# Loading K in 16 KB runs, and turning it in 1 KB pieces so that each batch comes out contiguous

## The chip, the core and the metric

The kernel runs on one core of one Trainium2 chip. The metric is the device time of one execution in microseconds (us), over repeated executions. Before the change it is 192.17 us, the median of three runs (192.04 to 192.22). The results are checked against the reference in every run.

## The reference

It is one decode step, one token for each of 4 batches, through two pairs of layers that share their weights: attention over a window of the cache, then a gated unit called GLU here.

```python
B, D = 4, 512;  Hq, Hkv, Sk, Dh = 32, 8, 8192, 128;  F = 1792      # all tensors bf16

def _A_ref(x, k_cache, v_cache, wq, wo):
    W = min(4096, max(256, Sk // 4))                               # 2048 positions
    q = (x @ wq) ...                                               # 4 query heads for each K/V head
    k = jnp.repeat(k_cache[:, :, Sk - W:, :], rep, axis=1)
    v = jnp.repeat(v_cache[:, :, Sk - W:, :], rep, axis=1)
    scores = jnp.einsum("bhqd,bhkd->bhqk", q, k) * (Dh ** -0.5)
    o = jnp.einsum("bhqk,bhkd->bhqd", _softmax(scores), v)
    return o ... @ wo

def _B_ref(x, w_gate, w_up, w_down):
    return (_sigmoid(x @ w_gate) * (x @ w_up)) @ w_down

x = x + _A_ref(_layernorm(x), ...);  x = x + _B_ref(_layernorm(x), ...)
x = x + _A_ref(_layernorm(x), ...);  x = x + _B_ref(_layernorm(x), ...)   # the same weights and caches
```

Two facts matter. The second attention needs the same K as the first, so K is loaded once (8 heads x 4 batches x 0.5 MB = 16.8 MB) and stays in SBUF. V is used twice; only its last few tiles can be kept, and the others are loaded twice.

## The kernel before

SBUF is one arena of 50 slots of 4 KB a partition. A slot holds one tile of 512 KB: K or V of one head and batch, or a piece of a weight. K takes 32 slots for good. The others are streaming buffers: SyncE issues the next load as soon as a slot comes free. A planner in Python fixes the order of the instructions on each engine. Each K tile is loaded in packets of 4 KB and turned in place on VectorE, 1024 four-byte words wide (one word is two bf16 values; the code lays K out in blocks of 32 words):

```python
def k_transpose(pairs):                    # pairs: one head, four batches = one "unit"
    for (h, b) in pairs:
        s = need(("K", h, b))
        v32 = slot_ap(s).bitcast(F32)                              # 128 x 1024 words
        P.op("vector", ..., lambda v, v32=v32: v.transpose(v32, v32),
             r=[("slot", s)], w=[("slot", s)])
```

TensorE reads the turned K with a step of 4 bytes, because both halves of each word stay together:

```python
    kt = slot_ap(ks[gi]).rearrange("p (j c k t) -> p c t j k", c=2, k=32, t=2)
    ... pe.matmul(ps[...], qbd[...], kt[:, cp // 2, cp % 2, :, :], ...)
```

The softmax then takes the maximum on VectorE, the exponential on ScalarE, reorders the result on TensorE and turns it on VectorE in one transpose of 128x256 words. The number of V tiles that stay from the first attention to the second is a constant:

```python
    KEEP_V = cfg.get("KEEP_V", 3)
    ...
    keep = set(seq[len(seq) - KEEP_V:])
```

A unit of the first attention turns the next K, multiplies q with K, does the softmax, multiplies with V, and frees the four V slots. SyncE fills them again.

Of the kernel before, what the change touches and what calls it, by code (L numbers as in the profile page):

```python
# [15 lines left out]
class _Op:  # L16
    __slots__ = ("idx", "eng", "name", "dur", "emit", "deps", "users", "start", "finish",
                 "sem", "val", "inc", "dma_bytes", "dma_rate", "waits", "prio", "ndeps_left")

    def __init__(self, idx, eng, name, dur, emit):  # L20
# [16 lines left out]
        self.ndeps_left = 0  # L37


class _Plan:  # L40
# [8 lines left out]
    def op(self, eng, name, dur, emit, r=(), w=(), banks=(), dma_bytes=0, dma_rate=0.0, after=()):  # L49
        o = _Op(len(self.ops), eng, name, dur, emit)  # L50
        o.dma_bytes = dma_bytes
# [32 lines left out]
def _schedule(ops, tm):  # L84
# [19 lines left out]
    while nleft:  # L104
        best = None
        best_key = None
        for e in ENGINES:
# [11 lines left out]
            for o in cand:  # L119
                t = ef  # L120
                for d in o.deps:
                    td = d.finish + sem_lat
                    if td > t:
                        t = td
                ests.append((t, o))
                if tmin is None or t < tmin:
                    tmin = t
            pick = None
            for x in ests:
                if x[0] <= tmin + tol and (pick is None or x[1].prio < pick[1].prio):  # L130
                    pick = x
            key = (pick[0], pick[1].prio)
# [114 lines left out]
class _SlotPool:  # L247
# [16 lines left out]
    bw_4k=412.0, bw_3k=409.0, bw_1k=356.0,  # L264
# [6 lines left out]
def build(nc, A_x, A_k, A_v, A_wq, A_wo, B_wg, B_wu, B_wd, out, cfg=None):  # L271
# [5 lines left out]
    KEEP_V = cfg.get("KEEP_V", 3)  # L277
# [20 lines left out]
    FCC = SLOT // D  # L298

# [12 lines left out]
    with es:  # L312
# [3 lines left out]
        arena = sb("arena", [128, NS * SLOT], BF16)  # L316
# [33 lines left out]
        pool = _SlotPool(NS)  # L350
        SB = (0, 1)
# [3 lines left out]
        CB = 7  # L355

        def slot_ap(s):
            return arena[:, s * SLOT:(s + 1) * SLOT]
# [4 lines left out]
        def c_act(n):  # L363
            return tm["act_fix"] + n * tm["act_el"]

# [13 lines left out]

        def take_load():  # L380
            name, emit = loads.pop(0)
# [4 lines left out]
        def fill():  # L386
            while loads and pool.free:
                take_load()

# [7 lines left out]

        def load_kv(name, cache, b, h):
            loads.append((name, lambda s: dma(str(name), slot_ap(s), kv_d(cache, b, h), w=[("slot", s)])))

        def load_cols(name, dram, n, rate):
            loads.append((name, lambda s: dma(str(name), slot_ap(s)[:, 0:n], dram, w=[("slot", s)], rate=rate)))

        def load_rows(name, dram, k, rate):
            loads.append((name, lambda s: dma(
                str(name), slot_ap(s)[:, 0:k * D].rearrange("p (f n) -> p f n", n=D), dram,
                w=[("slot", s)], rate=rate)))
# [47 lines left out]

        def add_weights(kind, k, only=None):
            chs = chunks[kind]
            if kind == "wq" and k:
# [170 lines left out]
        def k_transpose(pairs):  # L629
            for (h, b) in pairs:  # L630
                s = need(("K", h, b))
                v32 = slot_ap(s).bitcast(F32)
                P.op("vector", "T%d_%d" % (h, b), c_dve(1024), lambda v, v32=v32: v.transpose(v32, v32),  # L633
                     r=[("slot", s)], w=[("slot", s)])
# [3 lines left out]
        def softmax_unit(tag, pairs):  # L638
# [5 lines left out]
            ks = [where[("K", h, b)] for (h, b) in pairs]  # L644
            q_unit(tag, int(tag[0]), pairs[0][0], k2)

            def e_s(pe):
                last = None
                for cp in range(4):
                    for gi, (h, b) in enumerate(pairs):  # L650
                        kt = slot_ap(ks[gi]).rearrange("p (j c k t) -> p c t j k", c=2, k=32, t=2)
                        q0 = ((k2 * NB + b) * 4 + cp) * NR
                        last = pe.matmul(ps[32 * gi:32 * gi + NR, bank, :], qbd[:, q0:q0 + NR],  # L653
                                         kt[:, cp // 2, cp % 2, :, :], start=(cp == 0), stop=(cp == 3))
                return last
            P.op("tensor", "S" + tag, 16 * tm["pe_row"], e_s,
                 r=[("slot", s) for s in ks] + [("q", k2, a) for a in range(4)],
# [12 lines left out]
                 lambda a: a.activation(prow[:, :].rearrange("p (j k t) -> p j t k", k=32, t=2),  # L670
                                        ps[:, bank, :].rearrange("p (j t k) -> p j t k", k=32, t=2), ACTF.Exp, bias=nmax[:, 2 + k2:3 + k2], scale=1.0,
# [4 lines left out]
        def turn_p(tag, k2):  # L676
# [7 lines left out]
                 lambda v: v.transpose(ebuf[:, k2 * 256:(k2 + 1) * 256], prow[:, :].bitcast(F32)),  # L684
# [72 lines left out]
        def attn(L, gi_, wb):  # L757
# [6 lines left out]
            def front(ui):  # L764
# [3 lines left out]
                if L == 2:  # L768
                    for p in us[ui]:
                        done(("K",) + p)  # L770
# [22 lines left out]
        def glu(k, b0, b1):  # L793
# [181 lines left out]
```

## Time and profile before

| what | value | read from |
|---|---|---|
| time | 192.17 us (span of the profiled run 190.2) | the runs |
| DMA engines busy | 9 tenths in all slices but the first and the last | the span in 40 slices |
| main DMA queue | 72.37 MB, 97.9% of 16 engines' span | queue table |
| VectorE busy | 88.3 us, 46% | busy table |
| one K transpose, 1024 words | 1226 ns, 32 of them | groups |
| one softmax transpose, 256 words | 442 ns, 16 of them | groups |

These are lines of the profile's page of the kernel before. In the busy table each engine has its busy time, share and instructions. The digits are the busy tenths of 40 equal slices. The queue has packets, MB and its share of the 16 engines' span. The chain is what ended last, followed backwards. In the groups the columns are line, engine, operation, output<-input, shapes, count, then busy us and mean ns of one, then the idle us just before these instructions and what ended most of it.

```profile
...
PE 103.1 (54%) x1920; PEld 58.0 (30%) x1920; DVE 88.3 (46%) x220; ACT 33.3 (18%) x91; POOL 13.8 (7%) x73
...
DVE  6136998486582854729410023122584443311421
...
DMA  4999999999999999999999999999999999999990
...
q1 hardware_dynamic: 23392, 72.37, 97.9%
...
SPq 52%; DMA 29%; PE 10%; issue 4%; DVE 3%; ACT 2%; ACTq 0%
...
L718 PE MATMUL ps<-ebuf,arena 128*128 128x4 bf16 x1024 | 34.3, 167 | 15.6 <-DMA arena<-in_A_v_cache_dram 10.9
L633 DVE STREAM_TRANSPOSE arena<-arena 128x1024 f32<-128x1024 f32 x32 | 38.6, 1226 | 0.6 <-DMA arena<-in_A_k_cache_dram 0.2
...
L684 DVE STREAM_TRANSPOSE ebuf<-prow 128x256 f32<-128x256 f32 x16 | 7.1, 442 | 8.4 <-ACT prow L681 8.3
...
```

The DMA line and the queue's 97.9% say that the DMA engines are the bound. The chain agrees: 52% of it is SyncE's queue issuing loads and 29% is landings. TensorE's products with V (L718) wait 10.9 us for V to land.

### The profile page before, as it was taken

How to read it: one execution, taken by the hardware profiler on the slowest of the kernel's cores; microseconds unless marked ns; L12 is line 12 of the kernel's file. 1: busy time of each engine (PE TensorE's matmuls, PEld its weight loads, DVE VectorE, ACT ScalarE, POOL GpSimd, SP SyncE). 2: the span in 40 equal slices, each digit the busy share in tenths (PEclk: the TensorE clock that was granted, in tenths of full speed). 3: DMA queues.
4: the chain of work that ended last, by engine and by line, in shares of the span. 5: the costliest groups of instructions: out<-in, count | busy, mean ns of one | idle time of the engine just before them, and what ended most of it. 6: DMA issues, size and time to landing. Idle time of an engine off the chain costs nothing.

```text
span 190.2 us, 4466 instructions
## 1 busy us (share of the span) xinstructions
PE 103.1 (54%) x1920; PEld 58.0 (30%) x1920; DVE 88.3 (46%) x220; ACT 33.3 (18%) x91; POOL 13.8 (7%) x73
## 2 busy tenths in 40 slices
PE   0443322655517264171654436445979999966543
PEld 0110000232404123041234331321355555655122
DVE  6136998486582854729410023122584443311421
ACT  2010011430303003030020000000373333310100
POOL 3000001110101001010010000000022111100000
PEclk9999999999999999999999999999995555555555
DMA  4999999999999999999999999999999999999990
GB/s 133 344 416 410 408 410 389 409 394 404 407 390 411 391 405 412 388 409 394 400 393 389 407 405 371 397 337 409 409 409 408 402 410 406 408 408 405 403 365 16
DMA packets 23412, 72.66 MB, mean 382 GB/s; under 512 B 2264, under 2 KB 6368, under 8 KB 23392
## 3 DMA queue, kind: packets, MB, share of 16 engines
q1 hardware_dynamic: 23392, 72.37, 97.9%
q8 instruction: 15, 0.25, 0.5%
q14 instruction: 5, 0.04, 0.1%
HBM read 72.36 MB, written 0.00 MB: 381 GB/s over the span
## 4 chain that ended last, share of the span: by engine, by line
SPq 52%; DMA 29%; PE 10%; issue 4%; DVE 3%; ACT 2%; ACTq 0%
SPq L369 51%; DMA arena<-in_A_v_cache_dram 13%; DMA arena<-in_B_w_down_dram 11%; DMA arena<-in_A_wq_dram 5%; PE ps L653 3%; PE ps L718 2%; ACT prow L670 1%; PE ps L808 1%; PE ps L679 1%; PE ps L840 1%; DVE nmax L661 1%; PE ps L580 1%; PE ps L748 1%; DVE ebuf L684 0%; DVE ebuf L588 0%
## 5 line engine op out<-in xcount | busy, mean ns | idle before, releaser
L653 PE MATMUL ps<-arena,qbd 128*16 128x512 bf16 x256 | 28.7, 594 | 30.3 <-DVE arena L633 26.5
L718 PE MATMUL ps<-ebuf,arena 128*128 128x4 bf16 x1024 | 34.3, 167 | 15.6 <-DMA arena<-in_A_v_cache_dram 10.9
L633 DVE STREAM_TRANSPOSE arena<-arena 128x1024 f32<-128x1024 f32 x32 | 38.6, 1226 | 0.6 <-DMA arena<-in_A_k_cache_dram 0.2
L718 PEld LDWEIGHTS ps<-ebuf,arena 128*128 128x128 bf16 x1024 | 31.4, 104 | 23.8 <-DMA arena<-in_A_v_cache_dram 21.8
L670 ACT ACTIVATE prow<-ps,nmax 128x512 bf16<-128x512 f32 x16 | 13.3, 829 | 42.7 <-DVE nmax L667 41.3
L653 PEld LDWEIGHTS ps<-arena,qbd 128*16 128x16 bf16 x256 | 6.4, 109 | 44.1 <-DVE arena L633 27.1
L730 DVE TENSOR_TENSOR onb<-ps,rinv 128x16 bf16<-128x16 f32 x16 | 3.1, 192 | 35.5 <-PE ps L718 35.4
L661 DVE TENSOR_REDUCE nmax<-ps 128x1 f32<-128x512 f32 x16 | 10.9, 683 | 15.3 <-PE ps L653 15.3
L621 ACT CAST qbd<-ps 32x64 bf16<-32x64 f32 x32 | 6.5, 203 | 48.7 <-DVE qbd L618 48.4
L580 PE MATMUL ps<-arena,xn 128*4 128x512 bf16 x64 | 9.3, 576 | 9.4 <-DMA arena<-in_A_wq_dram 6.5
L688 POOL CAST s<-psm 128x1 bf16<-128x1 f32 x16 | 3.0, 187 | 146.9 <-ACT prow L670 146.9
L679 PE MATMUL ps<-prow,perm 128*128 128x512 bf16 x16 | 9.0, 563 | 5.4 <-ACT prow L670 5.2
L681 ACT CAST prow<-ps 128x512 bf16<-128x512 f32 x16 | 9.4, 586 | 9.5 <-PE ps L679 9.5
L684 DVE STREAM_TRANSPOSE ebuf<-prow 128x256 f32<-128x256 f32 x16 | 7.1, 442 | 8.4 <-ACT prow L681 8.3
L748 PE MATMUL ps<-onb,arena 128*128 128x4 bf16 x256 | 9.3, 166 | 2.9 <-DVE onb L730 1.5
L808 PE MATMUL ps<-arena,xn 128*4 128x448 bf16 x64 | 7.3, 556 | 6.4 <-DMA arena<-in_B_w_up_dram 3.5
L618 DVE CAST qbd<-ps 32x64 bf16<-32x64 f32 x32 | 6.8, 212 | 5.1 <-ACT qbd L621 3.8
L748 PEld LDWEIGHTS ps<-onb,arena 128*128 128x128 bf16 x256 | 8.2, 104 | 3.2 <-issue 2.9
L547 ACT ACTIVATE lnv<-lnv 128x4 f32<-128x4 f32 x4 | 0.8, 206 | 39.3 <-DVE lnv L544 39.3
L588 DVE STREAM_TRANSPOSE ebuf<-ps 128x512 f32<-128x512 f32 x4 | 2.9, 714 | 9.8 <-PE ps L580 9.8
L840 PE MATMUL ps<-hT,arena 128*128 128x4 bf16 x112 | 4.2, 167 | 4.3 <-DVE hT L830 2.2
L815 DVE STREAM_TRANSPOSE ebuf<-ps 128x448 f32<-128x448 f32 x4 | 2.6, 650 | 7.9 <-PE ps L808 7.9
(55 smaller groups left out, 61.8 us busy)
## 6 DMA issues: line engine op xcount, KB each, us to landing
arena<-in_A_v_cache_dram SPq DMA_DIRECT2D x61, 512.0 KB, 12.6
arena<-in_A_k_cache_dram SPq DMA_DIRECT2D x32, 512.0 KB, 13.1
arena<-in_A_wq_dram SPq DMA_DIRECT2D x16, 512.0 KB, 8.6
arena<-in_A_wo_dram SPq DMA_DIRECT2D x8, 512.0 KB, 15.0
arena<-in_B_w_gate_dram SPq DMA_DIRECT2D x8, 448.0 KB, 13.9
arena<-in_B_w_up_dram SPq DMA_DIRECT2D x8, 448.0 KB, 13.7
arena<-in_B_w_down_dram SPq DMA_DIRECT2D x6, 512.0 KB, 10.2
arena<-in_B_w_down_dram SPq DMA_DIRECT2D x2, 256.0 KB, 10.3
```

The lines of the kernel that those rows point to most:

```text
L369: o = P.op("sync", name, 0.0, lambda e, dst=dst, src=src: e.dma_start(dst, src), r=r, w=w, dma_bytes=nbytes, dma_rate=tm[rate])
L580: last = pe.matmul(ps[32 * hh:32 * hh + NB, qb, :], xn[:, c * NB:(c + 1) * NB], slot_ap(s)[:, hh * 512:(hh + 1) * 512], start=(c == 0), st ...
L633: P.op("vector", "T%d_%d" % (h, b), c_dve(1024), lambda v, v32=v32: v.transpose(v32, v32), r=[("slot", s)], w=[("slot", s)])
L653: last = pe.matmul(ps[32 * gi:32 * gi + NR, bank, :], qbd[:, q0:q0 + NR], kt[:, cp // 2, cp % 2, :, :], start=(cp == 0), stop=(cp == 3))
L661: lambda v: v.tensor_reduce(nmax[:, k2:k2 + 1], ps[:, bank, :], AXX, ALU.max),
L670: lambda a: a.activation(prow[:, :].rearrange("p (j k t) -> p j t k", k=32, t=2), ps[:, bank, :].rearrange("p (j t k) -> p j t k", k=32, t ...
L679: lambda pe: pe.matmul(ps[:, PB, :], perm[:, :], prow[:, :], start=True, stop=True),
L681: P.op("scalar", "pc" + tag, c_act(512), lambda a: a.copy(prow[:, :], ps[:, PB, :]), r=[("ppb",)], w=[("prow",)], banks=(PB,))
L684: lambda v: v.transpose(ebuf[:, k2 * 256:(k2 + 1) * 256], prow[:, :].bitcast(F32)),
L718: last = pe.matmul(ps[:, ob, gi * REP:(gi + 1) * REP], src[:, j * 128:(j + 1) * 128], ev[:, j % 2, j // 2, gi * REP:(gi + 1) * REP], start ...
L748: last = pe.matmul(ps[:, wb, c * nb:(c + 1) * nb], slot_ap(s)[:, r_ * D + c * 128:r_ * D + (c + 1) * 128], ov[:, o0:o0 + nb], start=(first ...
L808: last = pe.matmul(ps[32 * g:32 * g + NB, SB[n], 0:NF], xn[:, c * NB:(c + 1) * NB], slot_ap(s)[:, g * NF:(g + 1) * NF], start=(c == 0), st ...
```

## The change

The intent is fewer and longer packets. One DMA brings K of one head for all four batches, with 16 KB for each partition, instead of four DMAs of 4 KB each. A partition then holds 16 KB of one batch, and the batches alternate from partition to partition. Turned plainly, every row would hold the four batches mixed, word by word, and a product with K takes one batch at a time. So the transpose is cut into 16 pieces of 1 KB a partition (256 words), and each piece also sorts: it reads a piece in blocks of 32 words and writes it so that the batches are separated. It does not sort in place: every piece is written 1 KB below where it lies, onto the place that the previous piece was read from, and so the program makes each piece wait for the one before it. Next to this, the first load of wq comes in whole rows of 8 KB, four V tiles are kept instead of three, and the sigmoid moves to ScalarE.

```diff
-    KEEP_V = cfg.get("KEEP_V", 3)
+    KEEP_V = cfg.get("KEEP_V", 4)
@@ one DMA for K of a head
+            src = A_k[:, h, SK - W:SK, :].rearrange("b (p j) d -> p b (j d)", p=32)
+            dma("K%d" % h, arena[:, o:o + 4 * SLOT], src, w=[("kp", h, t + 1) for t in range(NKP)], rate="bw_16k")
@@ def k_transpose(pairs):
-            for (h, b) in pairs:
-                s = need(("K", h, b))
-                v32 = slot_ap(s).bitcast(F32)
-                P.op("vector", "T%d_%d" % (h, b), c_dve(1024), lambda v, v32=v32: v.transpose(v32, v32),
-                     r=[("slot", s)], w=[("slot", s)])
+            h = pairs[0][0]
+            need(("K", h))
+            for t in range(NKP):
+                src = kp_ap(h, t + 1).bitcast(F32).rearrange("p (j c k) -> p c j k", c=2, k=32)
+                dst = kp_ap(h, t).bitcast(F32).rearrange("p (c b x) -> p c x b", c=2, b=NB)
+                P.op("vector", "T%d_%d" % (h, t), c_dve(256), lambda v, dst=dst, src=src: v.transpose(dst, src),
+                     r=[("kp", h, t + 1)],
+                     w=[("kq", h, t)] + ([("kp", h, t)] if t else [("kp", h - 1, NKP)]))
@@ scores: step in K still 4 bytes
-                        kt = slot_ap(ks[gi]).rearrange("p (j c k t) -> p c t j k", c=2, k=32, t=2)
+                "p (t c b x q) -> p c q b t x", c=2, b=NB, x=32, q=2)
@@ softmax: p is written in another order, so its transpose reads gathered words
-                 lambda v: v.transpose(ebuf[:, k2 * 256:(k2 + 1) * 256], prow[:, :].bitcast(F32)),
+                 lambda v: v.transpose(
+                     ebuf[:, k2 * 256:(k2 + 1) * 256],
+                     prow[:, :].bitcast(F32).rearrange("p (y j x) -> p j x y", y=4, x=8)),
@@ first wq: whole rows
+                dma("wqr%d" % c, arena[:, o:o + 2 * SLOT], wq_d[:, c, :], ..., rate="bw_8k")
@@ sigmoid: 1 / (1 + e) as exp(-ln(1 + e))
-            P.op("vector", "gp1%d" % k, ... tensor_scalar(... 1.0, None, ALU.add) ...
-            P.op("vector", "grc%d" % k, ... reciprocal ...
+            P.op("scalar", "gln%d" % k, ... ACTF.Ln, bias=1.0 ...
+            P.op("scalar", "grc%d" % k, ... ACTF.Exp, scale=-1.0 ...
... (the planner's bookkeeping of the new places, a zero TensorE latency in the planner,
     and the last residual written straight as bf16 are left out)
```

In `dst` the innermost loop is over b, and neighbouring b lie 32 words, 128 bytes, apart.

More of the change, by code (lines that the diff above doesn't have):

```diff
@@ L17 @@
     __slots__ = ("idx", "eng", "name", "dur", "emit", "deps", "users", "start", "finish",
-                 "sem", "val", "inc", "dma_bytes", "dma_rate", "waits", "prio", "ndeps_left")
+                 "sem", "val", "inc", "dma_bytes", "dma_rate", "waits", "prio", "ndeps_left", "lazy")
     def __init__(self, idx, eng, name, dur, emit):
@@ L37, in __init__ @@
         self.ndeps_left = 0
+        self.lazy = 0.0
 class _Plan:
@@ L47, in __init__, with op @@
         self.bank_prev = {}
-    def op(self, eng, name, dur, emit, r=(), w=(), banks=(), dma_bytes=0, dma_rate=0.0, after=()):
+    def op(self, eng, name, dur, emit, r=(), w=(), banks=(), dma_bytes=0, dma_rate=0.0, after=(), lazy=0.0):
         o = _Op(len(self.ops), eng, name, dur, emit)
+        o.lazy = lazy
         o.dma_bytes = dma_bytes
@@ L121, in _schedule @@
                 for d in o.deps:
-                    td = d.finish + sem_lat
+                    td = d.finish + (0.0 if e == "tensor" and d.eng == e else sem_lat)
                     if td > t:
@@ L125, in _schedule @@
                 ests.append((t, o))
-                if tmin is None or t < tmin:
-                    tmin = t
+                if tmin is None or t + o.lazy < tmin:
+                    tmin = t + o.lazy
             pick = None
             for x in ests:
-                if x[0] <= tmin + tol and (pick is None or x[1].prio < pick[1].prio):
+                if x[0] + x[1].lazy <= tmin + tol and (pick is None or x[1].prio < pick[1].prio):
                     pick = x
-            key = (pick[0], pick[1].prio)
+            key = (pick[0] + pick[1].lazy, pick[1].prio)
             if best is None or key < best_key:
@@ L263 @@
     dma_issue=60.0, dma_lat0=900.0, dma_lat1=1100.0, dma_max_out=16,
-    bw_4k=412.0, bw_3k=409.0, bw_1k=356.0,
+    bw_16k=432.0, bw_8k=420.0, bw_4k=412.0, bw_3k=409.0, bw_1k=356.0,
     pe_pair=38.0, pe_small=230.0, pe_f32=450.0, pe_row=80.0, pe_sq=300.0,
@@ L298, in build @@
     FCC = SLOT // D
+    KP = SLOT // 4
+    NKP = 16
     x_d = A_x.rearrange("b s d -> (b s) d")
@@ L314, in sb @@
             return es.enter_context(nc.sbuf_tensor(name, shape, dt))
-        arena = sb("arena", [128, NS * SLOT], BF16)
+        arena = sb("arena", [128, NS * SLOT + KP], BF16)
         prow = sb("prow", [128, 512], BF16)
@@ L350, in build @@
         pool = _SlotPool(NS)
+        pool.free = list(range(4 * HKV, NS))
         SB = (0, 1)
@@ L357, in slot_ap @@
         def slot_ap(s):
-            return arena[:, s * SLOT:(s + 1) * SLOT]
+            o = s * SLOT + (KP if s >= 4 * HKV else 0)
+            return arena[:, o:o + SLOT]
         def c_dve(n, rate=None):
@@ L364, in c_act, with slot_tok @@
             return tm["act_fix"] + n * tm["act_el"]
+        def slot_tok(s):
+            return [("slot", s)] + ([("kq", s // 4, s % 4 * 4 + t) for t in range(4)] if s < 4 * HKV else [])
         def dma(name, dst, src, w, r=(), rate="bw_4k", nbytes=None, sem=None):
@@ L378, in build, with take_k @@
         where = {}
+        def take_k():
+            while loads and loads[0][0][0] == "K":
+                loads.pop(0)[1](None)
         def take_load():
+            take_k()
             name, emit = loads.pop(0)
@@ L386, in fill @@
         def fill():
+            take_k()
             while loads and pool.free:
                 take_load()
+                take_k()
         def need(name):
@@ L396, in done, with kp_ap, load_k @@
             pool.release(where.pop(name))
+        def kp_ap(h, t):
+            o = 4 * h * SLOT + t * KP
+            return arena[:, o:o + KP]
+        def load_k(h):
+            where[("K", h)] = h
+            o = 4 * h * SLOT + KP
+            src = A_k[:, h, SK - W:SK, :].rearrange("b (p j) d -> p b (j d)", p=32)
+            dma("K%d" % h, arena[:, o:o + 4 * SLOT], src, w=[("kp", h, t + 1) for t in range(NKP)], rate="bw_16k")
         def load_kv(name, cache, b, h):
-            loads.append((name, lambda s: dma(str(name), slot_ap(s), kv_d(cache, b, h), w=[("slot", s)])))
+            loads.append((name, lambda s: dma(str(name), slot_ap(s), kv_d(cache, b, h), w=slot_tok(s))))
         def load_cols(name, dram, n, rate):
-            loads.append((name, lambda s: dma(str(name), slot_ap(s)[:, 0:n], dram, w=[("slot", s)], rate=rate)))
+            loads.append((name, lambda s: dma(str(name), slot_ap(s)[:, 0:n], dram, w=slot_tok(s), rate=rate)))
         def load_rows(name, dram, k, rate):
@@ L406, in load_rows @@
                 str(name), slot_ap(s)[:, 0:k * D].rearrange("p (f n) -> p f n", n=D), dram,
-                w=[("slot", s)], rate=rate)))
+                w=slot_tok(s), rate=rate)))
         bounds = []
@@ L454, in build, with load_wq_rows, emit @@
                     last_use[(ch, v)] = k
+        def load_wq_rows(c):
+            def emit(s):
+                assert pool.alloc() == s + 1 and s >= 4 * HKV
+                where[(("wq", c, 1), 0)] = s + 1
+                o = s * SLOT + KP
+                dma("wqr%d" % c, arena[:, o:o + 2 * SLOT], wq_d[:, c, :], w=[("slot", s), ("slot", s + 1)],
+                    rate="bw_8k")
+            loads.append(((("wq", c, 0), 0), emit))
         def add_weights(kind, k, only=None):
+            if kind == "wq" and k == 0:
+                for c in range(NC):
+                    load_wq_rows(c)
+                return
             chs = chunks[kind]
-            if kind == "wq" and k:
+            if kind == "wq":
                 chs = chs[NC:] + chs[:NC]
@@ L643, in softmax_unit @@
             ob = OBS[k2]
-            ks = [where[("K", h, b)] for (h, b) in pairs]
+            hk = pairs[0][0]
+            ktv = arena[:, 4 * hk * SLOT:4 * (hk + 1) * SLOT].rearrange(
+                "p (t c b x q) -> p c q b t x", c=2, b=NB, x=32, q=2)
             q_unit(tag, int(tag[0]), pairs[0][0], k2)
@@ L650, in e_s @@
                     for gi, (h, b) in enumerate(pairs):
-                        kt = slot_ap(ks[gi]).rearrange("p (j c k t) -> p c t j k", c=2, k=32, t=2)
                         q0 = ((k2 * NB + b) * 4 + cp) * NR
                         last = pe.matmul(ps[32 * gi:32 * gi + NR, bank, :], qbd[:, q0:q0 + NR],
-                                         kt[:, cp // 2, cp % 2, :, :], start=(cp == 0), stop=(cp == 3))
+                                         ktv[:, cp // 2, cp % 2, b, :, :], start=(cp == 0), stop=(cp == 3))
                 return last
             P.op("tensor", "S" + tag, 16 * tm["pe_row"], e_s,
-                 r=[("slot", s) for s in ks] + [("q", k2, a) for a in range(4)],
+                 r=[("kq", hk, t) for t in range(NKP)] + [("q", k2, a) for a in range(4)],
                  w=[("pss", k2)], banks=(bank,))
@@ L669, in softmax_unit @@
             P.op("scalar", "ex" + tag, c_act(512) + 200.0,
-                 lambda a: a.activation(prow[:, :].rearrange("p (j k t) -> p j t k", k=32, t=2),
-                                        ps[:, bank, :].rearrange("p (j t k) -> p j t k", k=32, t=2), ACTF.Exp, bias=nmax[:, 2 + k2:3 + k2], scale=1.0,
+                 lambda a: a.activation(prow[:, :].rearrange("p (m x t) -> p m x t", x=8, t=2),
+                                        ps[:, bank, :].rearrange("p (m t x) -> p m x t", x=8, t=2), ACTF.Exp, bias=nmax[:, 2 + k2:3 + k2], scale=1.0,
                                         accum_out=psm[:, k2:k2 + 1]),
@@ L768, in front @@
                 if L == 2:
-                    for p in us[ui]:
-                        done(("K",) + p)
+                    for t in range(4):
+                        pool.release(4 * us[ui][0][0] + t)
                     fill()
@@ L791, in attn, with glu @@
                  r=[("psw", wb)] + [("xT", b) for b in g], w=[("xT", b) for b in g], banks=(wb,))
-        def glu(k, b0, b1):
+        def glu(k, b0, b1, last=False):
             nb = b1 - b0
@@ L822, in glu @@
                          r=[("e", 0), ("e", 1)], w=[("eg",)])
-            P.op("vector", "gp1%d" % k, c_dve(NH),
-                 lambda v: v.tensor_scalar(eg[:, 0:NH], eg[:, 0:NH], 1.0, None, ALU.add),
+            P.op("scalar", "gln%d" % k, c_act(NH),
+                 lambda a: a.activation(eg[:, 0:NH], eg[:, 0:NH], ACTF.Ln, bias=1.0),
                  r=[("eg",)], w=[("eg",)])
-            P.op("vector", "grc%d" % k, c_dve(NH) + 250.0,
-                 lambda v: v.reciprocal(eg[:, 0:NH], eg[:, 0:NH]),
+            P.op("scalar", "grc%d" % k, c_act(NH),
+                 lambda a: a.activation(eg[:, 0:NH], eg[:, 0:NH], ACTF.Exp, scale=-1.0),
                  r=[("eg",)], w=[("eg",)])
@@ L848, in glu @@
             xts = [("xT", b) for b in range(b0, b1)]
+            if last:
+                P.op("vector", "gres%d" % k, tm["dve_fix"] + 40.0,
+                     lambda v: v.tensor_tensor(xn[:, :], ps[:, CB, 128:128 + NX], xT[:, 0:NX], ALU.add),
+                     r=[("cb",)] + xts, w=[("xn",)], banks=(CB,))
+                return
             P.op("vector", "gres%d" % k, tm["dve_fix"] + 40.0,
@@ L860, in build @@
             us = units_of(g)
-            for (h, b) in us[0] + us[1]:
-                load_kv(("K", h, b), A_k, b, h)
+            for u in us[0:2]:
+                loads.append((("K", u[0][0]), lambda _, h=u[0][0]: load_k(h)))
             for ui, pairs in enumerate(us):
                 if ui + 2 < len(us):
-                    for (h, b) in us[ui + 2]:
-                        load_kv(("K", h, b), A_k, b, h)
+                    loads.append((("K", us[ui + 2][0][0]), lambda _, h=us[ui + 2][0][0]: load_k(h)))
                 hs = set(h for h, b in pairs)
@@ L892, in build @@
         g = GROUPS[-1]
-        glu(NG, g[0], g[-1] + 1)
+        glu(NG, g[0], g[-1] + 1, True)
         assert not loads
-        P.op("vector", "out_cast", tm["dve_small"], lambda v: v.tensor_copy(xn[:, :], xT[:, 0:NX]),
-             r=[("xT", b) for b in range(NB)], w=[("xn",)])
         def e_out_tr(pe):
```

## The prediction

> **What bounds the kernel.** The DMA engines. The span table shows them at 9 tenths in nearly every slice, near 410 GB/s; the queue table gives one queue 97.9% of 16 engines' span, for 72.4 MB. Of the chain of waits 52% is SyncE's queue issuing, 29% DMA landings. VectorE is busy 46%, TensorE 54%. So only bytes, DMA rate, starved stretches and the tail after the last landing count.
>
> **What the DMA gains.** In the packet records the median took 47 ns for 1 KB, 84 for 2 KB, 141 for 3.5 KB, 160 for 4 KB: about 9.3 ns plus 0.0368 ns a byte. Extended (an estimate), 8 KB takes 311 ns, 16 KB 612. [...] no 16 KB packet here shows it yet.
> - K, 16.8 MB: 40.96 us in 4 KB packets, 39.2 in 16 KB: -1.8 us.
> - First wq, 4.2 MB in 8 KB rows: -0.3.
> - 28 DMAs fewer, each with 16 completion packets of 9 ns: -0.25.
> - One V tile more is kept (4, not 3), 0.5 MB not read again: -1.3.
> - Tail: the last residual is written straight as bf16; one cast (0.17 us and its gap) goes: -0.2.
> Sum -3.85 us, all on the bound.
>
> **What it costs.** 32 transposes of 1226 ns become 128 of 128x256. The softmax's transpose of that size takes 442 ns; with each piece waiting for the one before I take 475. Per head 7.6 us instead of 4.9; VectorE in all from 88 to 106-110 us. [...] In the first attention a unit (one head, four batches) takes 11.7 us, paced by DMA; VectorE's work in it goes from 7.1 to about 10 us. It fits, barely: no cost, but VectorE nearly full from 20 to 100 us. The first scores move from 21.8 to about 28 us, before V arrives.
> Keeping the fourth V tile leaves 6 streaming buffers instead of 7 at the change from attention to GLU. There SyncE issued nothing from 107.3 to 115.05 us and the rate fell to 359-383 GB/s; one buffer fewer empties the queue 1.1 us earlier, most of it within the next issue's latency: +0.5 us (0.2 to 1.1).
> Sigmoid on ScalarE: add and reciprocal (0.19, 0.50 us) become two activations of 0.25, while w_up still lands: nothing..
>
> **Prediction: 188.8 us** (-1.7%), 187.2 to 190.8 in 8 of 10. Faster by over 2% (under 188.33): 0.37; within 2%: 0.58; slower: 0.05.
>
> **What would show it right.** Packets of 16 KB at 612 ns, 8 KB at 311; 60 V loads; over 415 GB/s where K lands; TensorE waiting for V landings, not transposes, before the products with V; transposes near 445 ns, 57-60 us; last w_down landing 3.3 us earlier; the dip at 114-118 us slightly deeper.
>
> **What would make it wrong.** Strided writes of the transposes, or the chain between pieces, costing 600 ns each: 12 us a unit, VectorE then paces the first attention, V buffers come free late, the DMA idles; up to 10 us slower. 16 KB packets split or no faster: 190.6. The slow start of each wq pass (packets of 250-300 ns for 2-3 us) vanishing with whole rows: 1 us faster. Deeper starvation at the layer change: 1 us slower.

Two remarks are cut where marked. Neither held a term of the sum: the gains still add up to 3.85 us, and with the 0.5 us for the lost buffer 192.17 becomes 188.8. The 475 ns are the author's estimate, the 442 ns of the page and an allowance of 33.

## More of the kernel before

The next view divides the first 136 us into stretches. The columns are the stretch, its length, the busy time of PE, PEld, DVE, ACT and POOL, the granted TensorE clock, the share of the DMA engines and GB/s. The first attention ends at 111 us; then comes GLU.

```profile
...
core 0: us, PE busy (x) PEld busy (x) DVE busy (x) ACT busy (x) POOL busy (x), PEclk, DMA share, GB/s
0.00:10.00 10.00, 2.62 (x18) 0.99 (x18) 3.77 (x15) 1.69 (x3) 1.74 (x9) 1.00 0.73 247
10.00:98.00 88.00, 39.56 (x677) 20.55 (x678) 55.89 (x97) 14.94 (x40) 6.04 (x32) 1.00 1.04 402
98.00:110.00 12.00, 5.22 (x147) 4.49 (x145) 0.53 (x3) 0.00 (x0) 0.00 (x0) 1.00 1.03 399
110.00:122.00 12.00, 6.05 (x84) 2.87 (x85) 3.67 (x14) 0.66 (x3) 0.00 (x0) 1.00 1.00 390
122.00:136.00 14.00, 8.62 (x110) 3.53 (x114) 3.94 (x17) 1.23 (x6) 0.00 (x0) 1.00 1.01 383
...
```

The rate is about 400 GB/s throughout, except at the start (247 GB/s). In the stretch from 10 to 98 us VectorE is busy 55.9 of 88 us.

VectorE has half the span free.

Its timeline shows what it waits for; the columns are start, busy us, engine, line and operation, count, and in brackets the idle time before and what ended it.

```profile
...
24.24 0.65 DVE L661 TENSOR_REDUCE nmax<-ps 128x1 f32<-128x512 f32 x1
...
31.05 0.63 DVE L661 TENSOR_REDUCE nmax<-ps 128x1 f32<-128x512 f32 x1
...
46.87 0.69 DVE L661 TENSOR_REDUCE nmax<-ps 128x1 f32<-128x512 f32 x1 [1.74 <-PE ps L653]
...
58.23 0.69 DVE L661 TENSOR_REDUCE nmax<-ps 128x1 f32<-128x512 f32 x1 [1.99 <-PE ps L653]
...
```

Each line is the maximum of one unit's scores. The second came 6.8 us after the first. Those at 46.87 and 58.23 are 11.4 us apart and VectorE stood idle before them: it had started late, worked faster than the loads, and caught up with them.

## The result, and the profile after

| | before | after |
|---|---|---|
| median, us | 192.19 (192.04 to 192.59, 4 runs) | 200.66 (200.36 to 202.08, 4 runs) |
| span of the profiled run, us | 190.2 | 198.5 |
| VectorE busy, us | 88.3 | 124.7 |

The change is slower: ratio 1.045, interval 1.040 to 1.051. A ratio here is the mean time of one kernel's fast runs over that of the other's fast runs of the same rounds, so it is not quite the ratio of the medians. The prediction was 188.8, with 190.8 as the upper end. It missed by some 12 us, on the other side of "before".

The lines of the page of the kernel after that answer to those above:

```profile
...
PE 99.7 (50%) x1920; PEld 56.4 (28%) x1920; DVE 124.7 (63%) x311; ACT 32.8 (17%) x95; POOL 13.9 (7%) x73
...
DVE  6116999999999999999999522112376445330231
...
DMA  5999999999999999999998470899999999999990
...
q1 hardware_dynamic: 19216, 71.84, 92.4%
...
DVE 49%; DMA 22%; PE 20%; issue 3%; SPq 3%; ACT 2%; DVEq 0%; ACTq 0%
...
L675 DVE STREAM_TRANSPOSE arena<-arena 128x256 f32<-128x256 f32 x128 | 79.0, 617 | 4.5 <-DMA arena<-in_A_k_cache_dram 0.8
L697 PE MATMUL ps<-arena,qbd 128*16 128x512 bf16 x256 | 28.7, 593 | 32.5 <-DVE arena L675 32.5
L764 PE MATMUL ps<-ebuf,arena 128*128 128x4 bf16 x1024 | 31.4, 166 | 8.0 <-DVE rinv L751 6.6
...
L728 DVE STREAM_TRANSPOSE ebuf<-prow 128x256 f32<-128x256 f32 x16 | 9.5, 593 | 7.9 <-ACT prow L725 7.8
...
```

The DMA engines fall to 4, 7, 0 and 8 tenths in the middle. VectorE stands at 9 from the fifth slice to the twenty-second. It now has 49% of the chain, where before it had 3%. The products with V (now L764) wait for VectorE and no longer for V. One K piece takes 617 ns in the record and 651 from one start to the next; the prediction took 475 for the latter. There is a second rise, at L728: the softmax's transpose, which now reads gathered words, went from 442 to 593 ns (m1 below times the gathered form by itself at 501 ns from start to start, the plain one at 334).

The same stretches as before:

```profile
...
core 0: us, PE busy (x) PEld busy (x) DVE busy (x) ACT busy (x) POOL busy (x), PEclk, DMA share, GB/s
0.00:10.00 10.00, 2.89 (x22) 0.92 (x22) 3.77 (x15) 1.69 (x3) 1.75 (x9) 1.00 0.77 304
10.00:98.00 88.00, 31.08 (x568) 16.39 (x568) 78.63 (x165) 11.46 (x34) 4.57 (x24) 1.00 1.02 410
98.00:110.00 12.00, 5.50 (x116) 3.49 (x116) 11.49 (x24) 1.36 (x3) 0.76 (x4) 1.00 0.91 317
110.00:122.00 12.00, 7.53 (x166) 5.42 (x166) 4.23 (x16) 1.44 (x4) 0.76 (x4) 1.00 0.46 156
122.00:136.00 14.00, 6.21 (x90) 3.19 (x90) 2.62 (x11) 1.08 (x5) 0.00 (x0) 1.00 0.80 279
...
```

Up to 98 us the loads are faster than before (304 against 247, then 410 against 402 GB/s). Then they starve: 317, 156 and 279 GB/s. The packets kept their median length (4 KB: 159 ns from 98 to 110 us, 162 before); the engines had too little to do, as the 16-engine share of 0.46 shows. VectorE's timeline shows why:

```profile
...
18.40 12.45 DVE L675 STREAM_TRANSPOSE arena<-arena 128x256 f32<-128x256 f32 x19 [0.80 <-DMA arena<-in_A_k_cache_dram]
30.88 0.69 DVE L705 TENSOR_REDUCE nmax<-ps 128x1 f32<-128x512 f32 x1
...
42.64 0.69 DVE L705 TENSOR_REDUCE nmax<-ps 128x1 f32<-128x512 f32 x1
...
54.41 0.69 DVE L705 TENSOR_REDUCE nmax<-ps 128x1 f32<-128x512 f32 x1
...
```

The first 19 pieces take 12.45 us, 0.66 us from one start to the next. The maxima come every 11.76 us, and VectorE does not wait before them. That pace is nearly the pace of the loads in the kernel before (11.7 us a unit). What is lost is the ability to catch up. Before, the first units took 6.8 to 8.4 us each, so a late start was made good by the fifth unit. After, the late start stays to the end: the last unit's scores begin at 110.95 us, where before they began at 91.61. TensorE's timeline at the end of the first attention, first of the kernel before and then of the kernel after, says what waits:

```profile
...
91.61 1.88 PE L653 MATMUL ps<-arena,qbd 128*16 128x512 bf16 x16 [4.80 <-DVE arena L633]
...
```

```profile
...
110.95 1.89 PE L697 MATMUL ps<-arena,qbd 128*16 128x512 bf16 x16 [1.50 <-DVE arena L675]
...
117.19 1.84 PE L764 MATMUL ps<-ebuf,arena 128*128 128x4 bf16 x64 [0.87 <-DVE rinv L751]
...
```

Since the products with V come late, V buffers come free late, and SyncE has no place to load into. These are SyncE's waits for buffers, before and after; the columns are who waited for what, us in all, times, and the longest.

```profile
...
SPq L369 <- PE ps L718: 11.3, 10, 2.4
...
```

```profile
...
SPq L378 <- PE ps L764: 25.0, 14, 8.1
...
```

Waits for the products with V rose from 11.3 to 25.0 us, one of them 8.1 us long.

To see how much each side weighs I added up the packet records. Packets of one size mostly took nearly the same time (nine in ten of those of 4 KB took 159 to 172 ns, before and after), so each size is counted with its median. The sum of these lengths over all packets, the short completion packets too (9 ns in the median), divided by 16 engines, is my estimate of the time that the loads need if they are never slowed or starved. What is missing in a stretch is called lost. The stretches of these sums are counted from the first packet, 1.7 us after the start of the span. This is my own sum over the trace, not a view of the profile.

| us | needed by the packets | lost 0-10 | lost 98-122 | lost 122-136 | lost in the last 10 before the last landing | first packet to last landing |
|---|---|---|---|---|---|---|
| before | 179.9 | 2.25 | 0.51 | 0.80 | 0.96 | 184.4 |
| after | 176.3 | 1.19 | 11.54 | 2.69 | 1.18 | 193.0 |

So the DMA side delivered: 3.6 us less is needed, and 1.1 us less is lost at the start. The starved stretch costs 12.9 us more. Together that is +8.5 us with the last ten us; from the first packet to the last landing it is +8.6, and the span grew by 8.3.

### The profile page after: what moved, and what is told of

Its sections match the earlier page's. It is cut to its first block, busy times and chain, and to the rows that moved or that the text cites. A ratio compares the mean times of both kernels' runs of the same rounds, so it can differ in the third digit from the quotient of the medians.

```text
span 198.5 us, 4530 instructions
## 1 busy us (share of the span) xinstructions
PE 99.7 (50%) x1920; PEld 56.4 (28%) x1920; DVE 124.7 (63%) x311; ACT 32.8 (17%) x95; POOL 13.9 (7%) x73
## 4 chain that ended last, share of the span: by engine, by line
DVE 49%; DMA 22%; PE 20%; issue 3%; SPq 3%; ACT 2%; DVEq 0%; ACTq 0%
DVE arena L675 40%; DMA arena<-in_B_w_down_dram 11%; DMA arena<-in_A_k_cache_dram 8%; PE ps L697 7%; PE ps L764 6%; DMA arena<-in_A_wq_dram 3%; DVE nmax L705 3%; SPq L378 3%; DVE ebuf L728 2%; PE ps L723 2%; PE ps L794 2%; PE ps L854 1%; ACT prow L714 1%; DVE qbd L658 1%; DVE rinv L751 1%
## 5 line engine op out<-in xcount | busy, mean ns | idle before, releaser
L675 DVE STREAM_TRANSPOSE arena<-arena 128x256 f32<-128x256 f32 x128 | 79.0, 617 | 4.5 <-DMA arena<-in_A_k_cache_dram 0.8
L764 PE MATMUL ps<-ebuf,arena 128*128 128x4 bf16 x1024 | 31.4, 166 | 8.0 <-DVE rinv L751 6.6
L764 PEld LDWEIGHTS ps<-ebuf,arena 128*128 128x128 bf16 x1024 | 29.8, 104 | 14.6 <-issue 14.5
L714 ACT ACTIVATE prow<-ps,nmax 128x512 bf16<-128x512 f32 x16 | 11.0, 687 | 86.6 <-DVE nmax L711 84.9
L728 DVE STREAM_TRANSPOSE ebuf<-prow 128x256 f32<-128x256 f32 x16 | 9.5, 593 | 7.9 <-ACT prow L725 7.8
L620 PE MATMUL ps<-arena,xn 128*4 128x512 bf16 x64 | 8.6, 596 | 8.2 <-DMA arena<-in_A_wq_dram 5.3
L854 PE MATMUL ps<-arena,xn 128*4 128x448 bf16 x64 | 6.7, 557 | 7.0 <-DMA arena<-in_B_w_up_dram 4.1
L861 DVE STREAM_TRANSPOSE ebuf<-ps 128x448 f32<-128x448 f32 x4 | 2.6, 651 | 10.1 <-PE ps L854 10.1
L723 PEld LDWEIGHTS ps<-prow,perm 128*128 128x128 bf16 x16 | 1.6, 102 | 16.2 <-ACT prow L714 15.4
```

Source lines behind the costliest of these rows:

```text
L620: last = pe.matmul(ps[32 * hh:32 * hh + NB, qb, :], xn[:, c * NB:(c + 1) * NB], slot_ap(s)[:, hh * 512:(hh + 1) * 512], start=(c == 0), st ...
L675: P.op("vector", "T%d_%d" % (h, t), c_dve(256), lambda v, dst=dst, src=src: v.transpose(dst, src), r=[("kp", h, t + 1)], w=[("kq", h, t)] ...
L714: lambda a: a.activation(prow[:, :].rearrange("p (m x t) -> p m x t", x=8, t=2), ps[:, bank, :].rearrange("p (m t x) -> p m x t", x=8, t=2 ...
L723: lambda pe: pe.matmul(ps[:, PB, :], perm[:, :], prow[:, :], start=True, stop=True),
L728: lambda v: v.transpose(ebuf[:, k2 * 256:(k2 + 1) * 256], prow[:, :].bitcast(F32).rearrange("p (y j x) -> p j x y", y=4, x=8)),
L764: last = pe.matmul(ps[:, ob, gi * REP:(gi + 1) * REP], src[:, j * 128:(j + 1) * 128], ev[:, j % 2, j // 2, gi * REP:(gi + 1) * REP], start ...
```

## The experiments

Three theories of the dear transposes were tested first. In the expectations, A says that the scattered writing (steps of 128 bytes) is dear by itself, B says that the chain of waits from piece to piece is dear, and C says that the loads landing in SBUF slow VectorE down. Another question, D in the expectations, is whether the fourth kept V tile and the lost buffers, not the transposes, starve the loads.

### m1_micro: transposes by themselves

A kernel of its own; its output is zeros. Sixteen transposes of 128x256 words are run in each form, with no loads under way. After them TensorE multiplies with K patterns of different steps. The lines are shortened; in every form each transpose also raises a semaphore, and "wait" is a wait for the transpose just before.

```diff
+for t in range(16): v.transpose(D(t), S(t))            # L55 plain to plain
+for t in range(16): v.transpose(D(t), rd(S(t)))        # L58 read in blocks, write plain
+for t in range(16): v.transpose(wr(D(t)), S(t))        # L61 read plain, write scattered
+for t in range(16): v.transpose(wr(D(t)), rd(S(t)))    # L64 both, as in the change, without a chain
+for t in range(16): v.transpose(D(t), gather(S(t+1)))  # L67 read gathered, as the softmax's after
+for t in range(16): v.transpose(S(t), S(t+1)); wait    # L70 plain, chained
+for t in range(16): v.transpose(wr(S(t)), rd(S(t+1))); wait   # L73 the change's pieces, chained
```

> This kernel computes nothing useful (its output is zeros, wrong on purpose). It issues 16 transposes of 128x256 fp32 in each of seven forms, each form from its own line, on an otherwise idle core, and then the 16 score products with the moving operand read in four patterns. Theory A (the access pattern costs, the chain does not): the plain form takes about 440 ns a piece also when every piece waits for the one before (under 500 ns from start to start), the forms that read in blocks or write scattered take 600 to 650 ns, chained or not. Theory B (the chain costs): the unchained form with the change's patterns takes about 440 ns, and the chained plain form 600 or more. Theory C (traffic of the DMA in SBUF slows the pieces): every form takes about 440 ns here. Products: if a step of 16 bytes in the moving operand costs TensorE nothing, all four patterns take the same 1.9 us for 16; if the step matters, the 16-byte form is longest.

One run, 85.23 us. This is VectorE's timeline; the second column is the time of sixteen.

```profile
...
10.25 5.34 DVE L55 STREAM_TRANSPOSE dst<-src 128x256 f32<-128x256 f32 x16
15.63 5.35 DVE L58 STREAM_TRANSPOSE dst<-src 128x256 f32<-128x256 f32 x16
21.01 7.18 DVE L61 STREAM_TRANSPOSE dst<-src 128x256 f32<-128x256 f32 x16
28.22 7.19 DVE L64 STREAM_TRANSPOSE dst<-src 128x256 f32<-128x256 f32 x16
35.45 8.02 DVE L67 STREAM_TRANSPOSE dst<-src 128x256 f32<-128x256 f32 x16
43.50 7.64 DVE L70 STREAM_TRANSPOSE src<-src 128x256 f32<-128x256 f32 x16
51.18 10.36 DVE L73 STREAM_TRANSPOSE src<-src 128x256 f32<-128x256 f32 x16
...
```

Divided by sixteen: plain 334 ns, reading in blocks 334, scattered writing 449, both 449, gathered reading 501. Chained, the plain form takes 477 and the change's form 647. So C falls, since the full 647 ns are there on an idle core. A and B each hold one part: scattered writing costs 115 ns alone (170 within the chain), and the chain costs 143 to 198 ns. Neither alone breaks the kernel, as x2 and x5 show below. The page's 442 ns for the softmax's transpose, my source, was a plain form, and its duration in the record is not the spacing in a chain (for the plain chained form of m1, 446 ns in the record and 477 from start to start). A semaphore was raised in all seven forms, so these 143 to 198 ns are not the raising's. Of TensorE's products, four took 0.43 us in the first 5 us, contiguous or with a step of 4 bytes, and 0.22 us after that with a step of 4 bytes; four with a step of 16 bytes, which came last, took about 0.9 us. The granted clock was 1.00 throughout.

### x1_inplace: no pieces at all

K still comes in 16 KB runs, but is turned in place, 1024 words wide, as before. TensorE picks the batch, with a step of 16 bytes instead of 4.

```diff
-            for t in range(NKP):
-                ... v.transpose(dst, src)                  # 256 words, one piece lower, sorted
+            for t in range(0, NKP, 4):
+                ... v.transpose(v32, v32)                  # 1024 words, in place
-                "p (t c b x q) -> p c q b t x", c=2, b=NB, x=32, q=2)
+                "p (n c e b q) -> p c q b n e", c=2, e=8, b=NB, q=2)
```

> The changed kernel with K still in 16 KB runs, but turned in place in 32 plain transposes of 128x1024; a batch is picked by TensorE reading every fourth pair (a step of 16 bytes in place of 4). A correct result is expected. Theory A (the pieces' cost on VectorE is the whole loss): VectorE goes back to about 88 us, the DMA no longer starves before the change of layer, and the time is 188 to 189.5 us, the gain forecast for DMA. Rival D (the loss comes from the buffers: 32 of 50 are now K's alone and one more V tile is kept): still above 196 us. If TensorE pays for the 16-byte step, the score products take longer than 1.9 us per 16 and the time is a few us above 189.

204.71 us (203.01 to 206.29), ratio 1.060 (1.052 to 1.067; one of its four runs was slow and is not in it). Two groups of its page:

```profile
...
L696 PE MATMUL ps<-arena,qbd 128*16 128x512 bf16 x256 | 62.1, 1090 | 27.6 <-DVE arena L675 24.0
L675 DVE STREAM_TRANSPOSE arena<-arena 128x1024 f32<-128x1024 f32 x32 | 37.3, 1209 | 1.1 <-DMA arena<-in_A_k_cache_dram 1.1
...
```

The transposes are back at 1209 ns, and the cost has gone to TensorE: a product with K takes 1090 ns where it took 594 before and 593 after. The granted clock also fell, to 0.73 in the stretch from 10 to 98 us where before it was 1.00, so the 1090 ns are not the step alone. Being above 196 us is also what D foretold, so this run does not decide between the transposes and the buffers; x3 does. This forecast missed, but the run shows why the change sorts the batches on VectorE: a plain layout with long runs is not free either.

### x2_plain_chain: the same chain, plain patterns

The 128 pieces stay, each one KB downwards and each waiting for the one before, but they are read and written plainly. The batches stay mixed, so the scores are wrong. It nevertheless passes the check, presumably because the scores are near zero and the softmax nearly uniform (not tested); the check cannot see this error.

```diff
-                src = kp_ap(h, t + 1).bitcast(F32).rearrange("p (j c k) -> p c j k", c=2, k=32)
-                dst = kp_ap(h, t).bitcast(F32).rearrange("p (c b x) -> p c x b", c=2, b=NB)
+                src = kp_ap(h, t + 1).bitcast(F32)
+                dst = kp_ap(h, t).bitcast(F32)
```

> The changed kernel with the same 128 chained transposes of 128x256, one KB downwards, but with plain patterns on both sides (wrong result on purpose: batches are mixed). Theory A (pattern): about 445 ns a piece, start to start under 500, a unit about 10 us, and the time 188 to 190 us. Theory B (chain or number of pieces): still about 617 ns a piece and about 200 us.

189.35 us (188.76 to 190.88), ratio 0.986 (0.980 to 0.992). Two groups of its page:

```profile
...
L675 DVE STREAM_TRANSPOSE arena<-arena 128x256 f32<-128x256 f32 x128 | 56.5, 442 | 4.3 <-DMA arena<-in_A_k_cache_dram 0.8
L764 PE MATMUL ps<-ebuf,arena 128*128 128x4 bf16 x1024 | 33.2, 166 | 20.6 <-DMA arena<-in_A_v_cache_dram 18.4
...
```

The pieces take 442 ns, with 480 from start to start, and the products with V wait for V again (18.4 us). This is the run that the prediction described: with pieces of 475 ns it had summed up to 188.8. So, given the chain, the access pattern alone makes the difference between 189.35 and 200.66 us (ratios 0.986 and 1.045); and of the pattern it is the writing, since in m1 reading in blocks took 334 ns, as did the plain form, and scattered writing 449 (in the chain it was not measured by itself).

### x3_keep3: three V tiles kept

```diff
-    KEEP_V = cfg.get("KEEP_V", 4)
+    KEEP_V = cfg.get("KEEP_V", 3)
```

> The changed kernel with three V tiles kept in place of four, so one streaming buffer more and 0.5 MB more to load. Theory A (VectorE paces the first attention): the transposes stay at 617 ns and the time stays within 1.5 us of the changed kernel's 200.6. Rival D (starved buffers): over 3 us faster than the changed kernel.

199.93 us (199.82 to 200.25), ratio 1.040 (1.036 to 1.044). The buffer given back, less the 0.5 MB more to load, is worth some 0.7 us here (the intervals of the two ratios overlap). D had asked for over 3 us, so the buffer is not what starves the loads.

### x5_two_down: pieces written two KB lower

Here the scattering stays and only the chain is loosened: a piece is written 2 KB lower, so it waits for the piece before the last and not for the last. The result passes the check, which, as x2 showed, would not see mixed batches. It needs 1 KB more of each partition, which a few small tiles give by sharing space (left out of the diff).

```diff
-        arena = sb("arena", [128, NS * SLOT + KP], BF16)
+        arena = sb("arena", [128, NS * SLOT + 2 * KP], BF16)
-                src = kp_ap(h, t + 1)...
+                src = kp_ap(h, t + 2)...
-                     r=[("kp", h, t + 1)],
-                     w=[("kq", h, t)] + ([("kp", h, t)] if t else [("kp", h - 1, NKP)]))
+                     r=[("kp", h, t + 2)],
+                     w=[("kq", h, t)] + ([("kp", h, t)] if t > 1 else [("kp", h - 1, NKP + t)]))
```

> The changed kernel with every piece written two KB downwards instead of one (three small tiles are folded into others to make room). A piece then overwrites what the piece two before it read, so it need not wait for the piece just before it. Patterns on both sides as in the change; the result is meant to be correct. The isolated measurement gave 449 ns from start to start without the chain and 647 with it. If both the scattered write and the chain count, as measured there: start to start 450 to 480 ns in runs of pieces, a unit about 9 to 10 us, no starved DMA before the change of layer, and 188.5 to 190.5 us, as the plain-pattern kernel (189.35). If the scattered write alone were the cause and the chain harmless: still above 600 ns and about 200 us.

190.52 us (189.08 to 191.43), ratio 0.989 (0.985 to 0.994). The pieces in the groups of its page:

```profile
...
L676 DVE STREAM_TRANSPOSE arena<-arena 128x256 f32<-128x256 f32 x128 | 60.1, 587 | 0.9 <-DMA arena<-in_A_k_cache_dram 0.8
...
```

The record still says 587 ns for a piece, hardly less than 617; read alone, it would say that nothing was gained. But the busy time of all 128, overlaps counted once, is 60.1 us where it was 79.0, and the start-to-start time is 442 ns. So these pieces, which do not wait for the last one, overlap: 587 ns long, they start 442 apart. The last transpose ends at 98.7 us instead of 110.9. It is enough to remove either half of the cost: plain patterns (x2) or a loose chain (x5).

### x8_folded_only: the control for x5

The small tiles share space as in x5, but the pieces go one KB down as in the change.

```diff
-        ones_f = sb("ones_f", [128, 128], F32)
+        ones_f = sb("ones_f", [128, 1], F32)
-        eg = sb("eg", [128, NFC * NB], F32)
+        eg = prow[:, 0:2 * NFC * NB].bitcast(F32)
... (hT and xc likewise share space with other tiles)
```

> A control: the changed kernel with the same small tiles folded into others as in the two-KB kernels, but pieces still written one KB downwards. If the fall from 200.7 to 190.5 us came from the chain being loosened, this is still 200 to 201 us with about 650 ns from start to start. If the folding did it, it is near 190.

201.94 us (201.69 to 202.84), ratio 1.051 (1.047 to 1.054), pieces at 616 ns. Sharing the space gains nothing, so x5's gain is that of the second KB.

### x7_two_down_keep3: x5 with three V tiles

```diff
-    KEEP_V = cfg.get("KEEP_V", 4)     # on top of x5
+    KEEP_V = cfg.get("KEEP_V", 3)
```

> The kernel before this one in the list, with three V tiles kept in place of four. It loads 0.5 MB more (1.28 us at 410 GB/s) and has one streaming buffer more at the change from attention to GLU. The forecast's terms were 1.3 us gained by the fourth tile and 0.5 us lost by the buffer: then this is 0.8 us slower than with four. If the lost buffer costs as much as the tile saves, the two are equal; if more, this is faster.

188.47 us (188.43 to 189.17), ratio 0.981 (0.979 to 0.983). It beats both kernels. Its stretches, with the columns as above:

```profile
...
0.00:10.00 10.00, 2.88 (x22) 0.92 (x22) 3.77 (x15) 1.69 (x3) 1.72 (x10) 1.00 0.76 304
10.00:98.00 88.00, 36.42 (x652) 19.32 (x652) 73.80 (x187) 12.81 (x37) 5.32 (x28) 1.00 1.02 410
98.00:110.00 12.00, 8.26 (x198) 6.12 (x198) 3.55 (x13) 1.36 (x3) 0.76 (x4) 1.00 1.04 400
110.00:122.00 12.00, 5.78 (x85) 2.57 (x85) 2.22 (x8) 1.16 (x5) 0.00 (x0) 1.00 0.96 356
122.00:136.00 14.00, 9.68 (x107) 3.14 (x107) 5.74 (x22) 3.00 (x11) 0.76 (x4) 1.00 1.02 405
...
```

The head start of the loads is the same as after (304 and 410 GB/s), and the starved stretch is nearly gone (400, 356 and 405 GB/s instead of 317, 156 and 279).

### x10_keep2: x5 with two V tiles

```diff
-    KEEP_V = cfg.get("KEEP_V", 4)     # on top of x5
+    KEEP_V = cfg.get("KEEP_V", 2)
```

> The two-KB kernel with two V tiles kept: another 0.5 MB to load (1.28 us) and another streaming buffer at the change of layer. With four kept it was 190.5, with three 188.5. If the starvation at 112 to 120 us is about buffers, this recovers up to the 1.5 us that three tiles still lose there and pays 1.28: 188 to 189.5. If the buffers are not the cause, 189.8.

190.83 us (190.70 to 191.36), ratio 0.992 (0.990 to 0.994). The packet sums of the three:

| V tiles kept | needed by the packets | lost 98-136 | lost in the last 10 | median us |
|---|---|---|---|---|
| 4 (x5) | 176.3 | 2.90 | 2.38 | 190.52 |
| 3 (x7) | 177.6 | 1.62 | 0.65 | 188.47 |
| 2 (x10) | 178.9 | 1.31 | 1.93 | 190.83 |

From three to four a tile saves 1.3 us of loads, and the starved stretch takes 1.28 back. From three to two 1.3 us more is loaded and only 0.31 won. By time three is the best of these, but the sums do not lay that to the tiles: between four and three the whole difference is in the last ten us (2.38 against 0.65 us lost), and between three and two more than half of it. That loss varies between 0.65 and 2.4 us from kernel to kernel with no pattern that I found; it stays open.

### x9_half_rows: x7 with the first wq in half rows

```diff
-            if kind == "wq" and k == 0:
-                for c in range(NC):
-                    load_wq_rows(c)
-                return
-            if kind == "wq":
+            if kind == "wq" and k:
```

> The best kernel so far (two KB downwards, three V tiles kept, 188.47 us) with the first wq loaded in half rows of 4 KB again, as in the kernel before. By packet lengths alone 0.3 us is lost. In the kernels with whole rows 0.5 MB more had landed 10 us after the first packet; if half rows are what makes the start of the wq pass slow, 1.2 to 1.6 us is lost: 189.7 to 190.1. If the slow start has another cause, 188.8.

190.53 us (189.67 to 191.20), ratio 0.990 (0.987 to 0.992). Its stretch from 0 to 10 us:

```profile
...
0.00:10.00 10.00, 2.63 (x18) 0.99 (x18) 3.77 (x15) 1.69 (x3) 1.72 (x10) 1.00 0.74 245
...
```

The first ten us move 245 GB/s, as in the kernel before, instead of 304, and 2.38 us are lost there instead of 1.19. By the packet sums, whole rows of the first wq are worth 1.2 us at the start, and the loads need 177.6 us with them and 178.0 without. The medians differ by 2.1 us (1.7 by the ratios; the two ran in different sessions); some of the rest lies between 122 and 136 us (0.51 us lost against none in x7), and is not explained. Why half rows start slowly is not shown.

### x4_small_parts: the small parts alone

The kernel before with four V tiles, the sigmoid on ScalarE, the last residual in bf16 and the planner's change, but without the new K and wq loads.

```diff
-    KEEP_V = cfg.get("KEEP_V", 3)
+    KEEP_V = cfg.get("KEEP_V", 4)
-            P.op("vector", "grc%d" % k, ... reciprocal ...
+            P.op("scalar", "gln%d" % k, ... ACTF.Ln, bias=1.0 ...
+            P.op("scalar", "grc%d" % k, ... ACTF.Exp, scale=-1.0 ...
... (and the bf16 residual and the planner's latency as in the change)
```

> The kernel before with only the small parts of the change: four V tiles kept, sigmoid on ScalarE, the last residual written straight as bf16, and the scheduler's latency between TensorE operations taken as zero. K, wq and the transposes as before. By the forecast's terms: 1.3 plus 0.2 us gained, 0.5 lost, so 191.2 us (190.4 to 191.7). If the fourth tile starves the DMA by as much as it saves: 192.

Median 193.24 us over six runs, of which three were slow (194.28 to 194.77) and one of these is the profiled one. The three fast runs (191.07, 192.12, 192.20) give a ratio of 0.997 (0.994 to 1.000). By that ratio the small parts gain some 0.6 us, with anything from 0 to 1.2 in the interval; the 1.0 that the prediction had given them (1.3 and 0.2 gained, 0.5 lost) is not ruled out. The slow runs show no lower clock than the fast ones (0.878 to 0.891 against 0.880 to 0.891), so this run settles little.

## Why the prediction was right or wrong

**Right: the bound, and what the DMA gains.** Packets of 16 KB took 614 ns (612 predicted), those of 8 KB 309 (311). There were 60 V loads. In the page's slices from 5 to 25 us, where K landed, the loads ran at 426 to 454 GB/s. The loads needed 3.6 us less, close to the sum of the first four terms (3.65). The extrapolation, 9.3 ns plus 0.0368 ns a byte, was fitted to this kernel's packets of 1 to 4 KB; the trace after agrees with it up to 16 KB.

**Wrong, and the cause of the miss: "with each piece waiting for the one before I take 475".** It took a plain transpose's duration, 442 ns, and an allowance of 33, an estimate. Measured were 647 ns from start to start on an idle core and 651 (median) in the kernel, so 10.4 us a head instead of 7.6. The allowance was in fact enough for the chain: a plain chained piece takes 477 to 480. What was missing is the scattered write, 170 ns a piece. The prediction's last paragraph named it ("Strided writes of the transposes, or the chain between pieces, costing 600 ns each ... V buffers come free late, the DMA idles; up to 10 us slower"), and that is what happened, but it was given a weight of 5%. The prediction rested on no timing of a scattered write; m1 gives one: in steps of 32 words, (449 - 334) / 256 = 0.45 ns more for a word without the chain.

**Wrong: "It fits, barely: no cost".** It took VectorE's work of a unit to be below the unit's time, 10 against 11.7 us. Even a fit as tight as the measured one (11.76 us, about the same as the loads' pace) was a cost here, because the first unit started late and VectorE, as full as it was, did not make up for it (the last unit's scores began at 110.95 us, before at 91.61). The prediction had seen the late start ("The first scores move from 21.8 to about 28 us"; they came at 28.91) and did not carry it to the end of the attention. Before, that lateness was gone by the fifth unit; after, it came out as 12.9 us of starved loads. This miss follows from the first: with pieces of 442 to 480 ns from start to start (x2, x5), and so units near the forecast 10 us while VectorE sets the pace, 2.9 us are lost from 98 to 136 us, against 14.2 in the change and 1.3 before.

**Mis-sized: the fourth V tile.** "+0.5 us" for the lost streaming buffer measured 1.28 (2.90 against 1.62 us lost, x5 and x7), so the tile gains nothing. By time, four are 2.1 us slower than three, but the sums put that difference in the last ten us, which is not explained.

**Mis-sized: the first wq.** "-0.3" was the packet length alone. The slow start vanished too, which the prediction had put among the things that could go wrong: 1.1 us after against before, 1.2 in x9 against x7.

**Not shown by itself: the sigmoid on ScalarE gains nothing.** Only the small parts together were run (x4), and their effect cannot be told from nothing. The exponential of the softmax, with its new order, fell from 829 to 687 ns; no run shows that this gained time.

With x2 the sum can be tested whole: when the pieces cost what was assumed, the time is 189.35 us against 188.8 predicted. The two mis-sized terms, the buffer (0.8 us too small) and wq (0.8 us too small on the other side), roughly cancel, so that it comes so close is partly luck.

## What to carry to other kernels

Cost an instruction with its own access pattern and its own wait: take the start-to-start time of a row of them, not the record's duration of a plain one (here 651 ns against 442). On an engine beside the bottleneck, ask not only whether the work fits in a unit but whether it is fast enough to make up for a late start, because here its lateness came back as buffers that came free late (SyncE waited 25.0 us for the products with V, before 11.3). And where each piece waited for the one before, one more piece of room (2 KB down instead of 1) was worth nearly as much here as a cheaper instruction: 10.1 us in x5, 11.3 in x2.
